# Products of q' with the carried state inside the attention run's row tiles, for six of twelve pairs

## Chip, cores and metric

The kernel runs on one core of one Trainium2 chip. The metric is device time in microseconds. Three runs of the kernel before the change gave 177.44 us (median), 176.88 us (lowest) and 177.53 us (highest).

## What is computed

A gated linear recurrence over four batches, eight heads, 768 steps and 48 columns per head, and then a two-layer network with a tanh GELU:

```python
for t in range(S):
    state = alpha[:, :, t, :, None] * state + einsum('bhd,bhe->bhde', k[:, :, t], v[:, :, t])
    y[:, :, t] = einsum('bhd,bhde->bhe', q[:, :, t], state)
x = y.transpose(0, 2, 1, 3).reshape(3072, 384)
out = gelu_tanh(x @ w_in) @ w_out          # w_in 384 x 2048, w_out 2048 x 384
```

## The kernel before

The sequence is cut into six chunks of 128 steps. A *pair* is one chunk of two batches, called units 0 and 1; there are twelve pairs, numbered 0 to 11 (pair m is chunk m // 2, batches 0 and 1 or 2 and 3). In a pair the recurrence becomes matrix products:

- `ln` (ScalarE) takes the logarithm of alpha, `cum` (TensorE, L378 and L380) sums it down the chunk, `b`, `binv` and `bend` (ScalarE, L407, L401) are exponentials of the sums and of their ends. `qp` = q·b and `kp` = k·binv (VectorE, L418) are q' and k'.
- q' and k' are transposed, by TensorE (L428) and a copy (`ev`, L446) in pairs 0 to 6 and by DMA from SP's queue (`turn`, L466) in pairs 7 to 11. The result `qkT` holds two heads on its 128 partitions: the even head of a couple on partitions 0 to 63, the odd one on 64 to 127.
- `attn` (L489) multiplies k' by q', one matmul for each head and unit. Each uses 64 rows of the array, the upper or the lower half, and the two halves alternate; 16 matmuls in a pair. `mask` (VectorE, L496) applies the triangle: four instructions in a pair, each one bank.
- `y` makes the result of one unit: for chunks after the first, four matmuls of 128 rows by 96 columns of q' with the carried state (L543), then eight of 48 columns of the masked products with v (L546), which add to the same bank. The state tile holds two heads on its partitions and two blocks of 48 columns, with zeros where head and block differ.
- `x` copies a unit's result out of PSUM (L553, on ScalarE or VectorE). It is transposed by TensorE (`tx`, L560, and `xe`, L564) or from pair 6 on by DMA (L472).
- `kv` (L506) and `st` (VectorE, L528 and L531) make the next state; the last chunk needs none.
- The network follows pair by pair: `l1` (layer 1, L572; eight steps of six matmuls, `hT`), `gelu` (ScalarE, L578) and `l2` (layer 2, L591; four steps of four matmuls for each unit, `acc`), `ot` (copy out, L603) and a store from SP's queue (L616). Exponentials and GELU need different tables in ScalarE, so there is a table load on either side of each pair's eight `gelu`.

PSUM's eight banks are shared out as `ca` (one buffer of two banks: `cum`, and the products of one unit in `attn`), `yk` (two banks: `y`, `kv` and everything that TensorE transposes) and `ff` (four banks, taken in turn: `hT`, `acc`, and the products of the other unit). A buffer is taken again only when its last reader has finished.

The order of each engine's instructions is fixed when the program is built. A planner in the kernel (class `Scheduler`) gives each task a cost, a priority and the buffers that it takes, and always puts the task next that can start first; the first part of the order is written out by hand (`FIRST`). TensorE, ScalarE, VectorE and the queues then run their lists strictly in order and wait by semaphores.

In the late part of the kernel, before the change, TensorE's list for one pair reads: seven `l1` steps of an earlier pair, `attn`, the eighth `l1` step, two `l2` steps, `y` of unit 0, one `l2` step, `y` of unit 1, one `l2` step, `cum` of the pair after the one of `attn`, four `l2` steps.

Of the kernel before, what the change touches and what calls it, by code (L numbers as in the profile page):

```python
# [7 lines left out]
F32 = mybir.dt.float32  # L8
# [38 lines left out]
class Scheduler:  # L47
# [16 lines left out]
    def order(self):  # L64
        free = {e: 0 for e in LAT}
        taken = {tag: [] for tag in self.bufs}
        table, wire, xbar, head, out = LN_EXP, 0, 0, 0, []
        left = {e: sorted((t for t in self.tasks if e in t.cost), key=lambda t: t.prio) for e in LAT}

        def given(tag):  # L70

            n, at = len(taken[tag]) - self.bufs[tag], 0
            for u in taken[tag][n] if n >= 0 else ():
                if u.done is None:
                    return None
                at = max(at, u.done)
            return at

        def ready(t, inorder=True):
            if inorder and t.stream not in (None, head):  # L80
                return None
            at = 0
            for d in t.deps:
                if d.done is None:
                    return None
                at = max(at, d.done)
            for tag, _ in t.takes:
                g = given(tag)
                if g is None:
                    return None  # L90
                at = max(at, g)
            return at

        def put(t, at, e):
            nonlocal wire, xbar
            for tag, users in t.takes:
                taken[tag].append(users)
            cost, lat = COST.get((e, t.kind), (t.cost[e], LAT[e])) if fixed and not 300 <= t.prio < 10000 else (t.cost[e], LAT[e])
            t.start, t.end, t.engine, t.load = at, at + cost, e, None
            free[e] = t.end  # L100
            t.done = t.end + lat
            if t.name in self.landed:
                t.done = self.landed[t.name]
                if e != "SP":
                    wire = t.done - W["receipt"]
            elif t.land is not None:
                wire = max(wire, t.end + W["lead"]) + t.land
                t.done = wire + W["receipt_hw" if e == "SP" else "receipt"]
            if t.kind in ("turn", "store"):
                xbar = t.done = max(xbar, t.end + W["landed"] - t.xbar) + t.xbar  # L110
                t.done += t.late
            out.append(t)

        def go(at, e, t):
            nonlocal table, head
            if e == "PE" and not fixed and self.fill and at < self.until and at - free[e] > 300:
                g = given("ff")
                n = int((at - max(free[e], g if g is not None else at) - 60) * 0.95 // W["fill"])
                if n > 0:
                    f = Task("fill", {"PE": n * W["fill"]}, 0, self.fill(n))  # L120
                    put(f.take("ff", f), max(free[e], g), e)
            put(t, at, e)
            if t.table not in (None, table):
                table = t.load = t.table
            for q in t.cost:
                left[q].remove(t)
            if t.stream is not None:
                head = min((x.stream for x in left["PE"] if x.stream is not None), default=None)

        fixed = True  # L130
        for step in self.first:
            e, name = step.split(":")
            if name[:5] == "fill.":
                n = int(name[5:])
                f = Task("fill", {"PE": n * W["fill"]}, 0, self.fill(n))
                at = given("ff")
                assert at is not None, "no bank for idle products"
                put(f.take("ff", f), max(free["PE"], at), "PE")
                continue
            e, t = {"P": "PE", "V": "DVE", "A": "ACT", "G": "POOL", "S": "SP"}[e], self.named[name]  # L140
            at = ready(t, False)
            assert at is not None, f"{name} can't go yet"
            go(max(at, free[e] + (W["table"] if t.table not in (None, table) else 0)), e, t)
        fixed = False
        while any(left.values()):
            best = None
            for e in LAT:
                found = []
                for t in left[e]:
                    at = ready(t)  # L150
                    if at is not None:
                        turn = W["table"] if t.table not in (None, table) else 0
                        at = max(at, free[e] + turn)
                        found.append((at, t, at - turn))
                if found:
                    window = min(f[2] for f in found) + 60
                    at, t, _ = min((f for f in found if f[2] <= window), key=lambda f: (f[1].prio, f[0]))
                    if best is None or at < best[0]:
                        best = at, e, t
            assert best is not None, "no task can go on"  # L160
            go(*best)
        return out
# [9 lines left out]
class _Kernel:  # L172
# [38 lines left out]
    TURN_QK, TURN_X = (7, 8, 9, 10, 11), (6, 7, 8, 9, 10, 11)  # L211

    EV_ACT = (0, 1, 2, 3)

    AT_FF, SINGLE = {0: (1,), 1: (), 2: ()}, (0, 1, 2)

# [254 lines left out]
    def turn_x_dma(self, u, i, c, b):  # L471
        return lambda e: self.nc.sync.dma_start_transpose(self.xT[c % self.NX][:, :, b, :], u["x", i])  # L472

    def attn(self, u, units, apart):
        nc, H, C = self.nc, self.H, self.C

        def emit(e):
            for i in units:
                if i in apart:
                    u["at", i] = [self.tile("ff", [C, H // 2, C], F32, "at") for _ in range(2)]  # L480
                else:
                    at = self.tile("ca", [C, 2, H // 2, C], F32, "at")
                    u["at", i] = [at[:, 0], at[:, 1]]
            for i in units:
                t, at = u["T"][:, :, i], u["at", i]
                for p in range(H // 2):
                    for o in range(2):
                        sl = slice(64 * o, 64 * o + 64)
                        nc.tensor.matmul(at[o][:, p, :], t[sl, 1, p, :], t[sl, 0, p, :], start=True, stop=True)  # L489
        return emit  # L490
# [44 lines left out]
    def y(self, u, i, c, b):  # L535
        nc, H, C, D = self.nc, self.H, self.C, self.D

        def emit(e):
# [6 lines left out]
            for h in range(H):  # L545
                nc.tensor.matmul(y[:, h, :], u["atm", i][:, h % 2, h // 2, :], u["vb"][:, i, h, :],  # L546
                                 start=c == 0, stop=True, skip_group_check=True)
        return emit

    def x(self, u, i):  # L550
# [66 lines left out]


    def tasks(self):
        s = self.s = Scheduler(self.BUFS, self.fill, 60000, self.FIRST, self.LANDED)  # L620
        B, NCH = self.B, self.NCH
        NP = B // 2
        self.p = {(c, i): {} for c in range(NCH) for i in range(NP)}
# [47 lines left out]
        for m, (c, i) in enumerate(pairs):  # L671
# [29 lines left out]
            for r, users in (("a", lns[m]), ("q", qp), ("k", kp)):  # L701
                loads[r, m, 0].take(r, *users)
            lns[m][0].take("la", *cums)
            if m - 1 in self.URGENT:
                cums[0].deps += ats[m - 1]
            if m in self.CUM_FF:
# [17 lines left out]
            for j in range(2):  # L724
# [17 lines left out]
                if m in self.SINGLE or j:  # L742
                    units = (j,) if m in self.SINGLE else (0, 1)
                    apart = self.AT_FF.get(m, (0,))
                    at = s.add("attn", {"PE": W["attn" if len(units) == 1 else "attn2"]}, o + 1, self.attn(u, units, apart), sum(turns[units[0]:], []))
                    ats.setdefault(m, []).append(at)
                    for w in units:
                        ms = masks[w] = [s.add("mask", {"DVE": W["mask"]}, P + 12 + 3 * w, self.mask(u, w, h), [at]) for h in range(2)]
# [4 lines left out]
            for j in range(2):  # L753
                b, o, k, ms, turned = 2 * i + j, P + 10 + 3 * j, kp[j], masks[j], turns[j]
                at = ats[m][-1 if m not in self.SINGLE else j]
                y = s.add("y", {"PE": W["intra"] + (W["inter"] if c else 0)}, P + 20 + j, self.y(u, j, c, b),
                          ms + turned + [vin[j]] + ([states[b, c - 1]] if c else []))
                xc = s.add("x", {"ACT": W["xc_act"], "DVE": W["xc"]}, P + 20 + j, self.x(u, j), [y])
                if m in self.TURN_X:
                    xe = tx = s.add("turn", {"SP": W["turn"]}, P + 22 + j, self.turn_x_dma(u, j, c, b), [xc], xbar=W["xbar_x"], late=W["late_x"] * (m < 6))  # L760
                else:
                    tx = s.add("tx", {"PE": W["tx"]}, P + 22 + j, self.turn_x(u, j), [xc])
                    xe = s.add("xe", {"DVE": W["xe"]}, P + 22 + j, self.turned_x(u, j, c, b), [tx])
                    tx.take("yk", xe)
                y.take("yk", xc)
                xc.take("x", tx)
                users += [at, y]
                ms[0].take("atm", y)
                xts[c, b], ys[b, c] = xe, y
# [1 line left out]
                if c < NCH - 1:  # L771
                    if u["packed"]:
# [2 lines left out]
                        tb.take("yk", k)  # L775
                        users.append(tb)
                        backs.append(tb)
                    kv = s.add("kv", {"PE": W["kv"]}, P + 30 + j, self.kv(u, j), [k, vin[j]])
                    st = states[b, c] = s.add("st", {"DVE": W["st" if c else "st0"]}, P + 30 + j, self.carry(u, j, c, b),
                                              [kv, end] + ([states[b, c - 1], ys[b, c - 1]] if c else []))  # L780
                    kv.take("yk", st)
# [139 lines left out]
```

## Time and profile before

| | before |
|---|---|
| median of three runs | 177.44 us (176.88 to 177.53) |
| span of the profiled execution | 175.3 us |
| TensorE busy | 170.4 us, 97% |
| ScalarE busy | 128.9 us, 74% |
| VectorE busy | 96.8 us, 55% |
| matmuls | 1845 |
| q' by state, L543, 128x96 | 80 matmuls, 6.7 us busy |
| masked products by v, L546, 128x48 | 192 matmuls, 8.7 us busy |
| attention products, L489, 64 rows, 128 columns | 192 matmuls, 8.0 us busy |

The profiled execution's own time is given as its span, 175.3 us from the first instruction to the last; the median of the runs is 2.1 us longer, for what lies around the span. Busy time of a matmul holds its way through the array, and matmuls overlap, so what a matmul costs TensorE's list is read from start to start in the timeline, not from its duration.

### The profile page before, as it was taken

The numbers are of one execution on the slowest core, as the hardware profiler recorded it, in microseconds if no ns is written. First come the engines' busy times: TensorE is split into PE (matmuls) and PEld (weight loads), VectorE is DVE, ScalarE is ACT, GpSimd is POOL, SyncE is SP. The second block draws the span as 40 slices with busy tenths as digits, with TensorE's granted clock in tenths as the row PEclk, the third lists the DMA queues.
The fourth block names the chain that finished last, engine by engine and source line by source line (L and its number), as shares of the span: only waits on it lengthen the run. The fifth ranks groups of instructions, "written<-read, shape, count | busy, mean of one in ns | idle before, by whom it ended". The sixth has DMA issues, their size and how long they took to land.

```text
span 175.3 us, 4440 instructions
## 1 busy us (share of the span) xinstructions
PE 170.4 (97%) x1845; PEld 135.4 (77%) x1845; DVE 96.8 (55%) x192; ACT 128.9 (74%) x213; POOL 57.7 (33%) x64
## 2 busy tenths in 40 slices
PE   7989999999999999999999999999999999999993
PEld 2667999667987896797798698698697697796973
DVE  6499920356888993795598897495426405000000
ACT  4677999666968668768788967977987984481941
POOL 2496348977645776576720000000000000000000
PEclk9999999999999999999999999999999999999999
DMA  4999999999999999999999992271271360401102
GB/s 138 307 262 224 210 243 238 246 205 207 249 273 204 242 256 220 217 226 199 200 264 224 200 136 80 54 172 52 47 187 28 90 165 4 115 20 49 45 0 90
DMA packets 49620, 28.86 MB, mean 165 GB/s; under 512 B 37696, under 2 KB 46016, under 8 KB 49600
## 3 DMA queue, kind: packets, MB, share of 16 engines
q0 software_dynamic: 26464, 17.70, 60.8%
q1 hardware_dynamic: 22592, 10.49, 24.8%
q10 hardware_dynamic: 544, 0.39, 0.8%
q8 instruction: 14, 0.23, 0.6%
q14 instruction: 6, 0.05, 0.1%
HBM read 25.17 MB, written 4.72 MB: 170 GB/s over the span
## 4 chain that ended last, share of the span: by engine, by line
PE 90%; DMA 6%; DVE 1%; issue 0%; ACT 0%; SPq 0%; POOL 0%
PE hT L572 36%; PE acc L591 36%; DMA v<-in_v_dram 4%; PE at L489 4%; PE qkT_ps L428 3%; PE yps L546 3%; PE kv L506 2%; PE yps L543 2%; DMA a<-in_alpha_dram 2%; PE cum L378 2%; PE xT_ps L560 1%; PE cum L380 1%; SPq L305 0%; ACT qkT L446 0%; DVE vb L389 0%
## 5 line engine op out<-in xcount | busy, mean ns | idle before, releaser
L572 PE MATMUL hT<-xT,w_in 128*128 128x256 bf16 x576 | 69.4, 273 | 0.0
L578 ACT ACTIVATE gT<-hT 128x512 bf16<-128x512 f32 x96 | 56.3, 600 | 17.7 <-PE hT L572 14.2
L591 PE MATMUL acc<-w_out,gT 128*128 128x384 bf16 (+3 forms) x416 | 69.0, 313 | 0.0
L572 PEld LDWEIGHTS <-w_in 128*128 128x128 bf16 x576 | 61.1, 114 | 1.6
L591 PEld LDWEIGHTS <-gT 128*128 128x128 bf16 x416 | 36.9, 98 | 19.2
L496 DVE TENSOR_TENSOR atm<-at,ut 128x512 bf16<-128x512 f32 x48 | 30.1, 681 | 12.7 <-PE at L489 12.6
L418 DVE TENSOR_TENSOR qp<-q,b 128x768 bf16<-128x768 f32 (+1 forms) x15 | 11.9, 794 | 14.0 <-ACT b L407 11.7
L418 DVE TENSOR_TENSOR kp<-k,binv 128x768 bf16<-128x768 f32 (+1 forms) x15 | 11.9, 791 | 10.6 <-ACT binv L407 10.6
L603 ACT COPY ot<-acc 128x384 f32<-128x384 f32 (+3 forms) x17 | 7.4, 439 | 13.0 <-PE acc L591 12.9
L308 POOL DMA_DIRECT2D k<-in_k_dram x11 | 12.2, 1107 | 6.6 <-DVE atm L496 3.0
L308 POOL DMA_DIRECT2D vb<-in_v_dram x11 | 12.1, 1102 | 6.7 <-PE hT L572 1.7
L308 POOL DMA_DIRECT2D q<-in_q_dram x11 | 12.2, 1109 | 6.1 <-DVE atm L496 1.3
L308 POOL DMA_DIRECT2D a<-in_alpha_dram x11 | 12.2, 1114 | 5.9 <-DMA w_in<-in_moe_w_in_dram 1.3
L407 ACT ACTIVATE b<-cum 128x768 bf16<-128x768 f32 (+1 forms) x15 | 10.3, 683 | 3.6 <-PE cum L380 2.3
L280 ACT ACT_TABLE_LOAD x9 | 11.5, 1283 | 0.9 <-PEq L905 0.7
L578 ACT ACT_TABLE_LOAD x9 | 11.5, 1283 | 0.2
L407 ACT ACTIVATE binv<-cum 128x768 bf16<-128x768 f32 (+1 forms) x15 | 10.2, 681 | 0.1
L528 DVE TENSOR_TENSOR stmp<-kv,st 128x384 f32<-128x384 f32 x16 | 8.8, 552 | 2.0 <-PE kv L506 2.0
L553 DVE CAST x<-yps 128x384 bf16<-128x384 f32 x12 | 6.7, 556 | 4.7 <-PE yps L546 4.7
L531 DVE TENSOR_TENSOR st<-stmp,ends 128x384 bf16<-128x384 f32 x16 | 8.9, 558 | 0.6
L446 ACT COPY qkT<-qkT_ps 128x512 bf16<-128x512 bf16 (+1 forms) x9 | 6.5, 728 | 3.7 <-PE qkT_ps L428 3.5
L546 PE MATMUL yps<-vb,atm 128*128 128x48 bf16 x192 | 8.7, 183 | 0.4 <-DVE vb L389 0.4
(65 smaller groups left out, 156.7 us busy)
## 6 DMA issues: line engine op xcount, KB each, us to landing
out_dram<-ot SPq DMA_DIRECT2D x19, 192.0 KB, 5.2
a<-in_alpha_dram POOLq DMA_DIRECT2D x9, 384.0 KB, 12.5
q<-in_q_dram POOLq DMA_DIRECT2D x9, 384.0 KB, 11.6
k<-in_k_dram POOLq DMA_DIRECT2D x9, 384.0 KB, 11.7
vb<-in_v_dram POOLq DMA_DIRECT2D x9, 192.0 KB, 11.6
w_in<-in_moe_w_in_dram POOLq DMA_DIRECT2D x4, 384.0 KB, 9.3
w_out<-in_moe_w_out_dram POOLq DMA_DIRECT2D x4, 384.0 KB, 11.1
out_dram<-ot SPq DMA_DIRECT2D x9, 96.0 KB, 1.8
```

What stands on the lines that cost most here:

```text
L280: nc.scalar.add_instruction(mybir.InstLoadActFuncSet(name=nc.get_next_instruction_name(), act_func_set_id=i, engine=mybir.EngineType.Activ ...
L308: dma(u[t][:, lo:hi].rearrange("t b h d -> t (b h) d"), src.rearrange("b h s d -> s (b h) d")[c * C:(c + 1) * C])
L407: self.nc.scalar.activation(u[n].rearrange("t i h d -> t i (h d)")[:, lo:hi], cum, AF.Exp, scale=1.0 if n == "b" else -1.0)
L418: self.nc.vector.tensor_tensor(out, rows, b, op=ALU.mult)
L496: self.nc.vector.tensor_tensor(u["atm", i][:, o], u["at", i][o], self.ut[:, None, :].to_broadcast([self.C, self.H // 2, self.C]), op=ALU.mult)
L528: nc.vector.tensor_tensor(s, acc, old, op=ALU.add)
L531: nc.vector.tensor_tensor(new.rearrange("f p (o d) -> f (p o) d", o=2), acc.rearrange("f p (o d) -> f (p o) d", o=2), ends, op=ALU.mult)
L546: nc.tensor.matmul(y[:, h, :], u["atm", i][:, h % 2, h // 2, :], u["vb"][:, i, h, :], start=c == 0, stop=True, skip_group_check=True)
L572: self.nc.tensor.matmul(h[:, s], w_in[:, j, nt % 4 + s], self.xT[c % self.NX][:, j, lo:hi].rearrange("p g t -> p (g t)"), start=j == 0, st ...
L578: return lambda e: self.nc.scalar.activation(self.gT[c % self.NG][:, nt:nt + 2, lo * self.C:hi * self.C], f.pop(("h", c, lo, nt)), AF.Gelu ...
L591: self.nc.tensor.matmul(f["acc", c, b][:, lo:hi], self.gT[c % self.NG][:, nt, b * self.C:(b + 1) * self.C], self.w_out[:, nt, lo:hi], star ...
L603: self.copy(e)(f["ot", c, b][:, sl], f["acc", c, b] if half is None else f["acc", c, b, half][:, sl])
```

## The change

In pairs 4, 5, 8, 9, 10 and 11 the products of q' with the carried state leave `y` and stand at the head of the `attn` run, for both units at once. They use half of the array's rows each, like the attention products, and multiply one head by its own 48 columns of the state; so four matmuls of 128 rows and 96 columns per unit become eight of 64 rows and 48 columns. Results of even heads go to one `yk` bank and those of odd heads to the other, both units side by side. `y` becomes one run of 16 matmuls that adds the masked products of both units; `x` copies one bank per instruction, that is, all even or all odd heads of both units, into a tile for the pair.

Around it: `attn` of these pairs takes both `yk` banks and waits for the states; `cum` of pairs 9, 10 and 11 goes ahead of `attn` of the pair before; `kv` of pairs 4 and 5 comes after `y`; the planner looks at the second buffer of a kind that a task takes, and stops putting idle matmuls in after 40 us of its own reckoning and not 60 us.

The order that results: nothing differs before `attn` of pair 4, and the number of idle matmuls is the same. TensorE's list for a late pair becomes: `attn` (with the 16 new matmuls ahead of its 16), five `l1` steps of the pair before, `y` of both units (16 matmuls), three `l1` steps, five `l2` steps, `cum`, three `l2` steps. In pairs 4 and 5 `attn` stands after the third `l1` step, the other five follow, then `y`, two `l2` steps, both `tx`, one `l2` step, both `kv`. `attn` of pair 11 comes two `l1` steps after `y` of pair 10, and `y` of pair 11 after one more `l1` step and four `l2` steps. On ScalarE one `x` copy now stands between the fifth and the sixth `gelu` in pairs 8 to 10, after the eighth in pairs 4 and 5, and between two `ot` in pair 11 (the other copy is VectorE's), and three `ot` copies move there from VectorE. The number of table loads is the same. On SP's queue transposes of x move behind those of q' and k' of the next pair.

```diff
+    CARRIED = (4, 5, 8, 9, 10, 11)
+    AHEAD = (9, 10, 11)
+    LATE_KV = (4, 5)
...
+    def carried(self, u, c, b):
+        nc, H, D = self.nc, self.H, self.D
+        u["y"] = [self.tile("yk", [self.C, 2, H // 2, D], F32, "yps") for _ in range(2)]
+        for i in range(2):
+            for p in range(H // 2):
+                for o in range(2):
+                    sl = slice(64 * o, 64 * o + 64)
+                    nc.tensor.matmul(u["y"][o][:, i, p, :], u["T"][sl, 0, i, p, :], self.state[b + i][c % 2][sl, p, o * D:o * D + D],
+                                     start=i == p == 0, stop=False, skip_group_check=True)
...
-    def attn(self, u, units, apart):
+    def attn(self, u, units, apart, carried=None):
...
+            if carried:
+                self.carried(u, *carried)
             for i in units:
                 t, at = u["T"][:, :, i], u["at", i]
...
+    def y_pair(self, u):
+        def emit(e):
+            for i in range(2):
+                for h in range(self.H):
+                    self.nc.tensor.matmul(u["y"][h % 2][:, i, h // 2, :], u["atm", i][:, h % 2, h // 2, :], u["vb"][:, i, h, :],
+                                          start=False, stop=True, skip_group_check=True)
+        return emit
+
+    def x_part(self, u, o):
+        def emit(e):
+            if "xs" not in u:
+                u["xs"] = self.tile("x", [self.C, 2, self.H // 2, 2, self.D], BF16, "x")
+                for i in range(2):
+                    u["x", i] = u["xs"][:, i].rearrange("t p o d -> t (p o d)")
+            self.copy(e)(u["xs"][:, :, :, o], u["y"][o])
+        return emit
...
-        s = self.s = Scheduler(self.BUFS, self.fill, 60000, self.FIRST, self.LANDED)
+        s = self.s = Scheduler(self.BUFS, self.fill, 40000, self.FIRST, self.LANDED)
...
+            if m in self.AHEAD:
+                for t in ats[m - 1]:
+                    t.deps += cums
...
-                    at = s.add("attn", {"PE": W["attn" if len(units) == 1 else "attn2"]}, o + 1, self.attn(u, units, apart), sum(turns[units[0]:], []))
+                    carried = (c, 2 * i) if m in self.CARRIED else None
+                    at = s.add("attn", {"PE": W["attn" if len(units) == 1 else "attn2"] + (230 if carried else 0)}, o + 1, self.attn(u, units, apart, carried),
+                               sum(turns[units[0]:], []) + ([states[2 * i + w, c - 1] for w in units] if carried else []))
...
+                if m in self.CARRIED:
+                    if j == 0:
+                        y = s.add("y", {"PE": 2 * W["intra"]}, P + 20, self.y_pair(u), masks[0] + masks[1] + vin + [at])
+                        xcs = [s.add("x", {"ACT": W["xc_act"], "DVE": W["xc"]}, P + 20 + o, self.x_part(u, o), [y]) for o in range(2)]
+                        at.take("yk", xcs[0]).take("yk", xcs[1])
...
-                    kv = s.add("kv", {"PE": W["kv"]}, P + 30 + j, self.kv(u, j), [k, vin[j]])
+                    kv = s.add("kv", {"PE": W["kv"]}, P + 30 + j, self.kv(u, j), [k, vin[j]] + ([y] if m in self.LATE_KV else []))
```

More of the change, by code (lines that the diff above doesn't have):

```diff
@@ L68, in order, with given @@
         left = {e: sorted((t for t in self.tasks if e in t.cost), key=lambda t: t.prio) for e in LAT}
-        def given(tag):
-            n, at = len(taken[tag]) - self.bufs[tag], 0
+        def given(tag, ahead=0):
+            n, at = len(taken[tag]) + ahead - self.bufs[tag], 0
             for u in taken[tag][n] if n >= 0 else ():
@@ L86, in ready @@
                 at = max(at, d.done)
-            for tag, _ in t.takes:
-                g = given(tag)
+            for k, (tag, _) in enumerate(t.takes):
+                g = given(tag, sum(x[0] == tag for x in t.takes[:k]))
                 if g is None:
                     return None
-                at = max(at, g)
+                at = max(at, given(tag) if tag == "ff" else g)
             return at
@@ L755, in tasks @@
                 at = ats[m][-1 if m not in self.SINGLE else j]
-                y = s.add("y", {"PE": W["intra"] + (W["inter"] if c else 0)}, P + 20 + j, self.y(u, j, c, b),
-                          ms + turned + [vin[j]] + ([states[b, c - 1]] if c else []))
-                xc = s.add("x", {"ACT": W["xc_act"], "DVE": W["xc"]}, P + 20 + j, self.x(u, j), [y])
+                if m in self.CARRIED:
[3 more added lines that the diff above has]
+                        at.take("yk", xcs[0]).take("yk", xcs[1])
+                else:
+                    y = s.add("y", {"PE": W["intra"] + (W["inter"] if c and m not in self.CARRIED else 0)}, P + 20 + j, self.y(u, j, c, b),
+                              ms + turned + [vin[j]] + ([states[b, c - 1]] if c else []))
+                    xcs = [s.add("x", {"ACT": W["xc_act"], "DVE": W["xc"]}, P + 20 + j, self.x(u, j), [y])]
+                    y.take("yk", xcs[0])
                 if m in self.TURN_X:
-                    xe = tx = s.add("turn", {"SP": W["turn"]}, P + 22 + j, self.turn_x_dma(u, j, c, b), [xc], xbar=W["xbar_x"], late=W["late_x"] * (m < 6))
+                    xe = tx = s.add("turn", {"SP": W["turn"]}, P + 22 + j, self.turn_x_dma(u, j, c, b), xcs, xbar=W["xbar_x"], late=W["late_x"] * (m < 6))
                 else:
-                    tx = s.add("tx", {"PE": W["tx"]}, P + 22 + j, self.turn_x(u, j), [xc])
+                    tx = s.add("tx", {"PE": W["tx"]}, P + 22 + j, self.turn_x(u, j), xcs)
                     xe = s.add("xe", {"DVE": W["xe"]}, P + 22 + j, self.turned_x(u, j, c, b), [tx])
                     tx.take("yk", xe)
-                y.take("yk", xc)
-                xc.take("x", tx)
+                if m in self.CARRIED:
+                    txs = (txs if j else []) + [tx]
+                    if j:
+                        xcs[0].take("x", *txs)
+                else:
+                    xcs[0].take("x", tx)
                 users += [at, y]
```

## The prediction

> **What bounds the kernel now.** I began with the clock and span, then the busy tenths and the chain that ended last on the page.
>
> ```profile
> PE   7989999999999999999999999999999999999993
> ...
> PEclk9999999999999999999999999999999999999999
> ...
> PE 90%; DMA 6%; DVE 1%; issue 0%; ACT 0%; SPq 0%; POOL 0%
> ```
>
> TensorE is busy in every slice after the first few at the full granted clock, and the chain is 90% its own work. A busy PE can still hide pauses, so the next view is its timeline over one late pair, in which every start can be set against the matmuls ahead of it.
>
> ```profile
> 127.48 4.75 PE L572 MATMUL hT<-xT,w_in 128*128 128x256 bf16 x42
> 132.16 0.62 PE L489 MATMUL at<-qkT 64*128 64x128 bf16 x16
> 132.71 0.84 PE L572 MATMUL hT<-xT,w_in 128*128 128x256 bf16 x6
> 133.40 1.46 PE L591 MATMUL acc<-w_out,gT 128*128 128x384 bf16 x8
> 134.70 0.33 PE L543 MATMUL yps<-st,qkT 128*128 128x96 bf16 x4
> 134.87 0.36 PE L546 MATMUL yps<-vb,atm 128*128 128x48 bf16 x8
> 135.07 0.81 PE L591 MATMUL acc<-w_out,gT 128*128 128x384 bf16 x4
> ...
> 136.74 0.49 PE L378 MATMUL cum<-la,ut_h 128*128 128x384 f16 x2
> ```
>
> Read start to start. Eight acc take 1.30 us (162 ns each), four products with the state 0.17 us (42 ns each), eight with v 0.20 us (25 ns each). Forty-two hT take 4.68 us; at the 109 ns that each costs elsewhere (18 in 1.96 us at 62.21) that is 0.10 us too much, the price of entering the half-row mode. Nothing else is left over: in this pair TensorE waits for nothing, and the same sums hold in the other pairs after 55 us. So the time changes by what TensorE's list gains or loses, plus any wait that is new.
>
> Two more places of the timeline say what the new matmuls may cost. The first pair of rows answers a window around 144.33 us, the second one around 144.42 us; the third shows one-column matmuls.
>
> ```profile
> 144.35 0.23 PE L489 MATMUL at<-qkT 64*128 64x128 bf16 x2
> ```
>
> ```profile
> 144.35 0.29 PE L489 MATMUL at<-qkT 64*128 64x128 bf16 x4
> ```
>
> ```profile
> 83.30 0.24 PE L380 MATMUL cum<-ones,la 128*128 128x1 f16 x4
> 83.40 0.32 PE L378 MATMUL cum<-la,ut_h 128*128 128x384 f16 x1
> ```
>
> A single such product lasts 216 to 227 ns, and two together take 0.23 us: the upper and the lower half start within a few ns of each other. The next two are done 0.06 us later. So couples follow each other at 56 ns (16 in 0.55 us, of which eight couples are 0.45 us and leaving the mode 0.10 us). One-column matmuls, by contrast, start every 25 ns, as the 48-column ones do: a floor that does not depend on size, but one that two halves of the array do not share, or the couple would not start together.
>
> **The change, part by part.**
>
> *Removed.* Eight products of 96 columns a pair: 2 x 0.17 = 0.335 us of TensorE's list, all on the path.
>
> *Added.* Sixteen products of half the rows and 48 columns, as eight couples. By the floor a couple takes 25 ns; by the trace's only half-row run 56 ns, but that is for 128 columns, and 48/128 of it is 21 ns. If halves did not overlap when this short, 16 x 25 ns = 0.40 us; if loading weights sets the 56 ns, 8 x 56 = 0.45 us. The ends are 0.17 and 0.45 us. I take 0.21 us (26 ns a couple), because the nearest rows are the 48-column run (same width, 25 ns) and the couple that starts together. They stand directly ahead of the 16 attention products in the same mode, so the entering and leaving, 0.10 us each, are paid once as before.
>
> A rule of the Trainium skill speaks against this: TensorEngine Tiling (Array Packing), Instruction Overhead, says that each matmul carries some 60 cycles whatever its width, and that one should not take a tiling factor from a dimension that is already small. Twice as many matmuls, all below 60 columns, would by that alone cost twice eight floors, an estimate of 0.40 us from that page; the trace has the same floor (25 ns at one column), but the row of two matmuls that start together is what I set against the rest.
>
> *y.* Two runs of eight with v (0.205 us each; the first after a wider one is a little dearer) become one run of 16, 16 x 25 = 0.40 us: 0.01 us less. That the banks alternate costs nothing in the attention run, which alternates banks too.
>
> *After attn.* In pairs 4 and 5 an hT now follows the half-row run where a kv did. Six hT behind such a run take 0.69 us (132.71 to 133.40), 0.03 us above 6 x 109 ns; twice, 0.06 us.
>
> *Moved on TensorE* (cum, kv, tx, l1 and l2 steps): no work added.
>
> *Copies.* x has the same 384 elements an instruction (0.56 us on VectorE, 0.48 us on ScalarE), now written in runs of 48. Price nothing on the path if the slack below holds.
>
> *New waits.* I walk one late pair from the end of its last hT, H (133.40 in the rows), with these rows of ScalarE:
>
> ```profile
> 133.60 0.60 ACT L578 ACTIVATE gT<-hT 128x512 bf16<-128x512 f32 x1 [0.73 <-PE hT L572]
> 134.21 1.28 ACT L280 ACT_TABLE_LOAD   x1
> 135.50 0.84 ACT L361 ACTIVATE la<-a 128x768 f16<-128x768 f32 x1
> ...
> 138.03 0.81 ACT L407 ACTIVATE binv<-cum 128x768 bf16<-128x768 f32 x1
> ...
> 138.86 1.28 ACT L578 ACT_TABLE_LOAD   x1
> ```
>
> ln ends at H+2.94. cum now stands behind five l2 steps, at H+3.25: 0.3 us of slack, which has to cover ScalarE's signal. cum ends at H+3.58, b starts 0.2 later, binv ends at H+5.3 (with bend, in one pair, H+5.5). attn starts at H+3.58+3x0.65 = H+5.53, and its second unit, which needs the buffer that cum held, 0.5 us later: 0.5 us of slack or more. The ot that came to ScalarE runs to H+6.2, the table load to H+7.5; the first hT, after attn, is done at about H+7.1, so the first gelu is some 0.2 us late. It has to be done when the fifth hT takes that bank, at H+9.0, and ends at H+8.1; gelu gains 0.05 us a step. VectorE does qp and kp until H+6.45, then four masks at 0.60 us: the first is out before the third hT wants its bank (H+7.1 against H+7.7), the last at H+8.9, and y comes at H+9.7. The x copy between two gelu (0.48 us) fits, since y's 0.40 us delays the next hT as well. Behind a waiting attn all of l1 would queue, and gelu behind that.
>
> Three tighter places: attn of pair 11 comes two l1 steps (1.3 us) after y of pair 10 and needs both yk banks; the later copy ends about 0.9 us after y. In pairs 4 and 5 the transposes of x need ScalarE's copy 1.3 us after y, out about 0.9 us after; the second kv follows the second xe by about 0.1 us. Losing that cover costs a tenth or two, once or twice. SP's queue: transposes of x are wanted a whole pair (12 us) later and take 1.2 us to issue and 2.3 us to land, so going behind q' and k' is free. Three ot leave VectorE, idle almost half of the time.
>
> *Sum.* Per pair 0.21 - 0.335 - 0.01 = -0.135 us; six pairs -0.81; plus 0.06: -0.75 us. The span of 175.3 us becomes 174.55, and the median, 2.1 us above it, 177.44 - 0.75 = 176.7 us. With a couple at 21 ns it is 176.45, with the halves one after the other 177.8, with 56 ns a couple 178.1.
>
> **Rivals.**
>
> *Halves do not gain* (the 0.40 or 0.45 us above): per pair +0.055 or +0.105 us, with the 0.06 together +0.4 to +0.7 us: 177.8 to 178.1 us. Against it: couples that start together. For it: no half-row run this short is in the trace, and every matmul loads its weights.
>
> *attn waits for its banks* (the slower side). It now needs both yk banks, two ff banks and ca at once, and in pairs 8 to 10 the next pair's cum holds ca until ScalarE has read it. ScalarE is busy 10.5 us of the 12.2 us pair (window 127.5 to 139.7) and gets one ot more, so if it falls behind, attn and everything behind it stand still. Slack is 0.5 us; beyond it each us late is a us in each of three pairs. It decides from about 0.25 us of waiting in each of the three (that eats the gain) and makes the kernel slower by over 0.5% from 0.55 us each, ScalarE over 1 us late. At 0.8 us each: +1.65, 179.1 us. For it: many tight places on one in-order list. Against: the walk finds none late.
>
> *The change does not shorten the list*: the products are not what a late pair waits on, ScalarE is, and saved time becomes idle: 177.4 us. Against it: ScalarE waits for hT today (0.73 us ahead of the gelu at 133.60).
>
> **How the numbers follow.** 0.5% is 0.89 us, about what a measurement of this kernel can tell from no change. The forecast has 0.70; its 0.75 us lies just inside that bound, and the 21 ns end or the runs' own spread (0.65 us over three) puts about 0.30 of this beyond it, 0.40 inside. Halves without gain 0.12, all within 0.5%. No shortening 0.04. Waits 0.14, slower. Together faster 0.30, same 0.56, slower 0.14. The range leaves out the waits and little else: from 176.2 (the 21 ns end less 0.25 us of spread) to 178.2. The forecast's own range is 176.2 to 177.1.
>
> **What would show it.** After the change the timeline should show 16 yps of 64 rows by 48 columns in about 0.21 us, then the 16 at, and l1 after 0.55 us; 16 yps in 0.40 us later; no idle time of TensorE in pairs 4 to 11; pairs 9 to 11 about 0.13 us shorter than 12.2 us. A gap ahead of at or of the first yps shows the second rival; 0.40 us for the first 16 shows the first. A gain of more than 1.1 us would mean that something other than these products got cheaper, and I have not seen it.

## The result, and the profile after

| | before | after |
|---|---|---|
| median of ten runs each, side by side | 177.29 us (176.88 to 179.56) | 178.57 us (177.8 to 182.48) |
| ratio | | 1.0071 [1.0046, 1.0095] |
| span of the profiled execution | 175.3 us | 176.0 us |

The change makes the kernel slower by 0.7%; 178.57 us lies above the top of the forecast range, 178.2 us. The profiled execution of the changed kernel was the fastest of its ten (177.8 us), so its profile shows the loss at its smallest, and the run of 182.48 us is not counted in the ratio. In every run of the record the time is 1.8 us above its own span; the 2.1 us given ahead of the prediction compared the profiled execution with the median of others.

First the page after: TensorE's row of the busy tenths, and the chain that ended last.

```profile
PE   7799999999999999999999899999999999999992
...
PE 88%; DMA 6%; ACT 4%; issue 0%; DVE 0%; DVEq 0%
```

One slice in the middle has fallen to 8, and ScalarE has entered the chain. Before going there, the timeline of TensorE over a late pair, with the columns start, duration, engine, line, operation, tiles, shapes and count.

```profile
126.83 0.37 PE L488 MATMUL yps<-st,qkT 64*128 64x48 bf16 x16
127.04 0.61 PE L508 MATMUL at<-qkT 64*128 64x128 bf16 x16
127.58 3.47 PE L608 MATMUL hT<-xT,w_in 128*128 128x256 bf16 x30
130.88 0.56 PE L573 MATMUL yps<-vb,atm 128*128 128x48 bf16 x16
```

Start to start, the sixteen new products take 0.21 us, the attention run 0.54 us, `y` 0.41 us. The next pair's products start at 138.88, so the pair lasts 12.05 us; before, from 127.48 to 139.67, it lasted 12.19 us. That is the forecast's gain of some 0.13 us. The time must have been lost elsewhere. The timeline around 100 us, after and then before:

```profile
97.92 2.76 PE L627 MATMUL acc<-w_out,gT 128*128 128x384 bf16 x16
101.59 0.81 PE L608 MATMUL hT<-xT,w_in 128*128 128x256 bf16 x6 [0.92 <-DMA xT<-x]
```

```profile
98.20 2.76 PE L591 MATMUL acc<-w_out,gT 128*128 128x384 bf16 x16
100.80 0.82 PE L572 MATMUL hT<-xT,w_in 128*128 128x256 bf16 x6
```

The sixteen `acc` need 2.60 us start to start before, 3.67 after: 1.07 us are lost waiting for `xT<-x`. These six `hT` are layer 1's first step for pair 6, the first pair whose x is transposed by DMA. The chain, cut to the stretch that ends there:

```profile
96.35 5.20 DMA xT<-x
101.55 0.04 issue
101.59 0.49 PE hT L608 x3
```

The second unit's transpose was issued at 96.35 us and landed 5.20 us later. Before, it was issued at 96.44 and landed 3.80 us later, at 100.24, and TensorE wanted it at 100.80: 0.56 us of slack. Issued no later, landed 1.3 us later.

The DMA view from 99.4 to 101.8 us says why. It has 40 slices of 0.06 us; the row is what all queues moved in each.

```profile
GB/s 294 282 514 265 273 286 260 269 273 282 77 4 0 0 0 0 0 0 0 4 4 9 9 9 9 13 4 13 9 13 9 9 13 137 273 290 303 273 294 290
...
q8 instruction: 1, 0.02, 2.8%
```

The transposes run at some 270 GB/s. At 99.56 us one packet of 16,384 bytes comes in on q8, the queue that loads instructions (the spike of 514). Its record lasts about 1.05 us. From 100.05 us on nothing moves for half a microsecond, then some 10 GB/s, and only from 101.4 us on the full rate, although the transposes are unfinished: a halt of about 1.4 us. Before the change this stretch holds no such packet; it comes 3 us later, at 102.59 us, and the window from 102.4 to 105.2 us (slices of 0.07 us) shows the same halt:

```profile
GB/s 59 7 234 0 0 29 117 241 271 274 271 274 263 88 18 0 0 0 0 0 0 0 0 7 11 7 7 11 7 11 11 7 11 7 80 263 289 293 293 293
...
q8 instruction: 1, 0.02, 3.2%
```

The short pause around the spike is that between two transposes; the next one, that of k' of pair 8, starts at 102.8 us, stops at 103.4 and goes on at 104.8. It takes 4.45 us from issue to landing instead of some 2.75, and nobody waits for it. So the halt is not new; its place is.

Before, the packets follow each other at every 249 TensorE instructions on average (210 to 292 from one to the next). Up to this point the changed kernel has 32 more of them (8 more matmuls in each of pairs 4 and 5, each with its weight load). This packet starts at TensorE's 2259th instruction before and at its 2237th after, of which 32 are new, so it meets work that lies 54 instructions, or 3 us, earlier. The packets do not all move alike: the next one starts 1.4 us later than before the change (112.5 against 111.1), the fourteenth 5.5 us earlier (156.6 against 162.1). In all there are 48 more matmuls, and fifteen packets where there were fourteen. The last comes at 172.3 us, among the last stores. The DMA view from 172 to 176 us, after and then before (slices of 0.1 us):

```profile
GB/s 338 338 256 0 0 0 0 0 146 315 292 169 16 8 8 8 15 8 0 0 87 287 236 46 0 123 174 31 0 0 0 0 0 0 0 0 0 0 0 0
```

```profile
GB/s 0 0 0 0 0 92 300 346 215 31 0 0 0 97 287 226 46 0 120 180 28 0 0 0 0 0 0 0 0 0 0 0 0 0 0 0 0 0 0 0
```

The pause ahead of the store of 96 KB is in both. But after the change this store ends in a trickle of some 8 GB/s from 173.2 to 173.8 us, and lands 2.4 us after its issue, not 1.6. From the last `ot` copy to the end of the span it takes 2.86 us, against 2.44 before.

So the account is: the matmuls −0.81 us up to pair 10 (whose first `hT` starts at 151.53 before and 151.80 after, that is −0.81 + 1.08; read directly, 0.28 of it ahead of the sixteen `acc` above and 0.52 behind pair 6's first `hT`), the wait for x of pair 6 +1.08, the last stores +0.42: +0.69 us, where the spans differ by 0.68.

### The profile page after: what moved, and what is told of

It is laid out like the page before. It is cut to its first block, busy times and chain, and to the rows that moved or that the text cites. A ratio compares the mean times of both kernels' runs of the same rounds, so it can differ in the third digit from the quotient of the medians.

```text
span 176.0 us, 4532 instructions
## 1 busy us (share of the span) xinstructions
PE 169.3 (96%) x1893; PEld 134.1 (76%) x1893; DVE 94.7 (54%) x188; ACT 129.6 (74%) x217; POOL 57.8 (33%) x64
## 4 chain that ended last, share of the span: by engine, by line
PE 88%; DMA 6%; ACT 4%; issue 0%; DVE 0%; DVEq 0%
PE hT L608 36%; PE acc L627 33%; PE qkT_ps L434 4%; PE at L508 4%; DMA k<-in_k_dram 3%; DMA xT<-x 3%; PE cum L384 2%; PE kv L525 2%; PE yps L573 1%; ACT L286 1%; PE yps L565 1%; PE xT_ps L596 1%; PE yps L488 1%; PE yps L562 1%; ACT qkT L452 1%; PE k_ps L460 1%
## 5 line engine op out<-in xcount | busy, mean ns | idle before, releaser
L627 PE MATMUL acc<-w_out,gT 128*128 128x384 bf16 (+3 forms) x416 | 67.8, 313 | 0.0
L639 ACT COPY ot<-acc 128x384 f32<-128x384 f32 (+3 forms) x20 | 8.8, 443 | 15.6 <-PE acc L627 15.6
L367 ACT ACTIVATE la<-a 128x768 f16<-128x768 f32 (+1 forms) x11 | 8.5, 785 | 0.1
L583 DVE CAST x<-yps 128x384 bf16<-128x384 f32 x6 | 3.3, 557 | 8.7 <-PE yps L573 8.7
```

Of the source, the lines that this page charges most:

```text
L367: self.nc.scalar.activation(u["la"][:, lo:hi, :, 0:self.D], u["a"][:, lo:hi], AF.Ln)
L627: self.nc.tensor.matmul(f["acc", c, b][:, lo:hi], self.gT[c % self.NG][:, nt, b * self.C:(b + 1) * self.C], self.w_out[:, nt, lo:hi], star ...
L639: self.copy(e)(f["ot", c, b][:, sl], f["acc", c, b] if half is None else f["acc", c, b, half][:, sl])
```

## Experiments

The expectations number the theories and say what each holds. The account above, that the added instructions move the instruction packets onto transfers that TensorE is about to need (Theory 3 in them), was formed only after the first four runs; those ask where the wait arises. Each kernel was timed in five rounds beside the kernel before on the same chip.

**The same kernel again**, to see whether the wait is always there.

> The changed kernel once more (one comment more), for a second profile and ten more times. Theory 1 (the transposes of x of pair 6 land late by DMA, TensorE waits ahead of the first layer-1 step of pair 6, and the 0.3 us saved in pairs 4 and 5 is lost there): again 178 to 179 us, and a gap of TensorE of 0.5 to 2.5 us at about 100 us, no other gap over 0.1 us. Theory 2 (the new order of the late pairs brings waits that the first profile did not catch, since its run was the fastest of ten): gaps after 110 us.

178.49 us against 177.30, ratio 1.0049 [1.0018, 1.0081]. The wait is there again and larger, 1.40 us start to start, with the packet at 99.5 us and the landing at 101.4.

**Only the late pairs**: the new products in pairs 8 to 11, none in 4 and 5.

```diff
-    CARRIED = (4, 5, 8, 9, 10, 11)
+    CARRIED = (8, 9, 10, 11)
-    LATE_KV = (4, 5)
+    LATE_KV = ()
```

> Only pairs 8 to 11 have the products inside the attention run; pairs 4 and 5 are as before the change. Theory 1: the place at 100 us is as before the change, with no gap or one under 0.3 us, and four pairs at 0.135 us less make it 0.5 us faster than before, 176.8 us. Theory 2: the late pairs' waits stay, 178 to 178.5 us.

176.49 us against 177.30, ratio 0.9949 [0.9918, 0.9979]: faster than both kernels. The timeline at the place of the wait shows none:

```profile
97.82 2.76 PE L627 MATMUL acc<-w_out,gT 128*128 128x384 bf16 x16
100.42 0.82 PE L608 MATMUL hT<-xT,w_in 128*128 128x256 bf16 x6
```

With no instruction added ahead of pair 6 the packet is at 102.4 us, as before the change, and x lands at 100.4. From pair 4's `attn` to pair 10's first `hT` TensorE's list takes 89.54 us instead of 90.05: 0.52 us less, where four pairs at 0.135 make 0.54. There are fourteen packets, and none at the end. The median falls by 0.81 us, more than the list does; the ratio's interval, 0.37 to 1.45 us, holds both.

**Only pairs 4 and 5.**

```diff
-    CARRIED = (4, 5, 8, 9, 10, 11)
-    AHEAD = (9, 10, 11)
+    CARRIED = (4, 5)
+    AHEAD = ()
```

> Only pairs 4 and 5 have them; pairs 8 to 11 are as before the change. Theory 1: 0.3 us saved ahead of 98 us, a gap of 0.3 us or more at about 100 us, so no gain: 177.3 to 178.3 us. Theory 2: no new waits, 0.2 us faster than before, 177.1 us.

178.47 us against 177.30, ratio 1.0046 [1.0014, 1.0077], a little above the range expected. TensorE waits 0.83 us for pair 6's x, landing at 101.4 with the packet at 99.4. These two pairs alone make the kernel slower, although the spot where it shows lies after them.

**Pair 6's x through TensorE**, as in pairs 0 to 5, in the changed kernel.

```diff
-    TURN_QK, TURN_X = (7, 8, 9, 10, 11), (6, 7, 8, 9, 10, 11)
+    TURN_QK, TURN_X = (7, 8, 9, 10, 11), (7, 8, 9, 10, 11)
```

> The changed kernel, but x of pair 6 is transposed by TensorE and a copy, not by DMA: 6 matmuls of 128 columns more on TensorE's list, 0.33 us. Theory 1: the gap at 100 us is gone, and the six pairs' 0.75 us less 0.33 us is left: 176.9 us. Theory 2: the waits of the late pairs stay, 178 us or more.

177.70 us against 177.30, ratio 1.0027 [1.0000, 1.0054]. The wait at 100 us is gone, but the gain is not what Theory 1 expected. The timeline shows where it went:

```profile
103.33 0.62 PE L508 MATMUL at<-qkT 64*128 64x128 bf16 x16 [1.22 <-DMA qkT<-kp]
```

`attn` of pair 7 now waits for its transposed k'; the packet lies at 101.2 us, among those. (The profiled execution took 179.05 us, so its wait may be longer than that of most.) The transfers of pair 6 were only the first to be hit: putting the wait down to them was half right. Between 99 and 170 us the timelines of these four kernels mark no other idle time of TensorE, so none of the waits is for a bank or a copy.

**Moving the packet without the change.** The first try replaced the first seven idle matmuls of 512 columns by 23 of 156, in the kernel before, as 32 more TensorE instructions at the same number of columns.

```diff
-            for _ in range(n):
-                self.nc.tensor.matmul(ps, self.zero[:, 0:self.C], self.zero, start=True, stop=True)
+            k, w = (23, 156) if n == 7 else (n, 512)
+            for _ in range(k):
+                self.nc.tensor.matmul(ps[:, 0:w], self.zero[:, 0:self.C], self.zero[:, 0:w], start=True, stop=True)
```

> The kernel before the change, but the first seven idle matmuls (512 columns each) are 23 of 156 columns: 32 more instructions on TensorE's list (16 weight loads, 16 matmuls) in time that is idle anyway, all else the same. Pairs 4 and 5 of the changed kernel add just as many ahead of pair 6. Theory 3 (the 16 KiB packet of the instruction queue at 102.6 us comes about 3 us earlier, as it does after the change, and the transposes of x of pair 6 land 1.2 us later for it): slower by 0.8 to 1.2 us, 178.1 to 178.5 us, with a gap of TensorE at about 101 us. Theory 1 as first stated (TensorE merely arrives earlier than the transposes, which go at the pace of the loads): no change, 177.3 us.

178.33 us against 177.16, ratio 1.0065 [1.0048, 1.0082], but not for the reason that was to be tested: the start lost 2.2 us, so TensorE came to pair 6 after its x (1.9 us later than before, at 102.66 us). The second `cum` run of the start, before and in this kernel:

```profile
5.83 1.06 PE L346 MATMUL cum<-la,ut_blk 128*128 128x384 f16 x7
```

```profile
6.43 1.44 PE L347 MATMUL cum<-la,ut_blk 128*128 128x384 f16 x7 [0.54 <-ACT la L360]
```

TensorE waited for `la`, which ScalarE could start at 5.86 us and not at 5.04, when its alpha had landed; the next step came 1.24 us after the start of these seven in place of 0.90, and the first attention run at 10.97 us in place of 8.76. Whether the narrower idle matmuls had a part in the late load isn't shown, and the profiled execution (178.96 us) is the longest of the six. As a test of Theory 3 this run says nothing.

**More idle matmuls in the changed kernel**: 71 of 48 columns, and 39 of 92, in place of the seven (the same lines, other numbers).

> The changed kernel, but the first seven idle matmuls are 71 of 48 columns: 128 more instructions on TensorE's list at the start, which moves the instruction packets by half their distance of some 11 us, away from the transposes of x of pair 6. Theory 3: packets at about 89 and 106 us, the gap at 100 us under 0.3 us, and the gain that the sum gave comes through: 176.4 to 176.8 us. Theory 1 as first stated: the gap stays, 178 us or more. The start may be up to 0.4 us later, since narrow matmuls may not run at the rate of wide ones.

177.59 us against 177.16, ratio 1.0015 [0.9988, 1.0043]. No wait at 100 us, but in the profiled execution (179.01 us, the longest of the twelve) the start is nearly 3 us late, so TensorE comes after the landing in any case. How much the packet's place gave can't be told.

> The same with 39 of 92 columns, 64 more instructions. Theory 3: the packet comes about 4 us ahead of where the changed kernel has it, at about 95 us, when the transposes of x of pair 6 are on their way too; its hold of about 1 us may fall on the loads still under way or on the transposes, so 176.5 to 178 us, and the landing of the second transpose of x, less where the packet came, says which. Theory 1: as the changed kernel, 178.5 us.

178.12 us against 177.16, ratio 1.0049 [1.0027, 1.0071], just above the range expected. Here the start is as usual, and the packet, at 97.9 us, lies on the same transposes:

```profile
102.16 0.60 PE L609 MATMUL hT<-xT,w_in 128*128 128x256 bf16 x4 [1.35 <-DMA xT<-x]
```

Moving the packet by 1.7 us was not enough to clear them.

**Moving the packet where it costs nothing.** Idle matmuls at the start were the wrong place. The sixteen layer-2 matmuls of one unit (chunk 1, batch 0), in the kernel before, become two of 192 columns each: 32 more TensorE instructions for about 0.04 us, well ahead of pair 6, and all else as it was.

```diff
+            halves = (c, b) in ((1, 0),)
+            if halves:
+                for nt in range(part * 4, part * 4 + 4):
+                    for lo in (0, 192):
+                        self.nc.tensor.matmul(f["acc", c, b][:, lo:lo + 192], self.gT[c % self.NG][:, nt, b * self.C:(b + 1) * self.C],
+                                              self.w_out[:, nt, lo:lo + 192], start=nt == 0 and lo == 0, stop=nt == self.NFT - 1,
+                                              skip_group_check=True)
...
```

> The kernel before the change, with each of the 16 layer-2 matmuls of one unit (chunk 1, batch 0, run at about 52 to 57 us) split in two of 192 columns: 32 more instructions on TensorE's list at the price of some 0.05 us, the start left alone. Pairs 4 and 5 of the changed kernel add as many. Theory 3 (the 16 KiB packet of instructions then falls at about 99.5 us instead of 102.6 us and holds the transposes of x of pair 6 back): slower by 0.8 to 1.2 us, about 178.3 us, a gap of TensorE at about 100.8 us of 0.5 us or more. Theory 1 as first stated (only how early TensorE arrives counts): no change, 177.2 us.

178.31 us against 177.29, ratio 1.0068 [1.0042, 1.0094]. The products are those of the kernel before, and the loss is about as large as that of the change. That the two ratios nearly agree is chance: this kernel has neither the 0.81 us gained nor the longer tail. Timeline, then the DMA view from 99.4 to 101.8 us:

```profile
98.51 2.44 PE L598 MATMUL acc<-w_out,gT 128*128 128x384 bf16 x14
101.78 0.49 PE L572 MATMUL hT<-xT,w_in 128*128 128x256 bf16 x3 [0.83 <-DMA xT<-x]
```

```profile
GB/s 282 277 307 290 286 245 533 269 269 286 265 269 269 154 9 0 0 0 0 0 0 0 0 4 9 9 9 9 9 9 13 9 9 9 13 13 111 273 286 299
```

The packet has come 3 us earlier, to 99.76 us, and the transposes stop behind it until 101.6 us. This is the run that shows Theory 3: nothing but these sixteen matmuls, 32 instructions more, was changed, and TensorE is as early at pair 6 as before (its sixteen `acc` start at 98.18 us, before at 98.20).

The same in the kernel with only the late pairs (same lines, L634 in place of L598):

> The kernel with the products inside the attention run in pairs 8 to 11 alone (176.5 us), with one unit split, 32 more instructions. Theory 3: the packet at 99.5 us again, a gap at about 100.5 us, 177.4 to 178 us. Theory 1: no change, 176.5 us.

178.11 us against 177.29, ratio 1.0053 [1.0035, 1.0070]: the fastest kernel has lost its gain to 32 instructions.

```profile
101.91 0.27 PE L608 MATMUL hT<-xT,w_in 128*128 128x256 bf16 x1 [1.33 <-DMA xT<-x]
```

**Moving it further.** Four units split (chunk 1, all batches), 128 more instructions, in the kernel before and in the changed one.

> The kernel before the change with four units (chunk 1) split like this, 128 more instructions. Theory 3: packets move by half their distance, away from the transposes of pair 6, so no gap; 64 more matmuls cost 0.1 to 0.2 us: 177.2 to 177.4 us. Theory 1: the same.

179.33 us against 177.29, ratio 1.0120 [1.0097, 1.0142], a miss. Packets now lie at 96.7, 128.9 and 143.3 us, each on transposes that are wanted soon: 0.71 us are lost ahead of pair 6's layer 1, and 0.83 and 0.75 us ahead of `attn` of pairs 10 and 11. One of these:

```profile
133.71 0.45 PE L489 MATMUL at<-qkT 64*128 64x128 bf16 x10 [0.77 <-DMA qkT<-kp]
```

The expectation had looked at one packet. All of them move.

> The changed kernel with the same four units split, 128 more instructions. Theory 3: the packet moves from 99.5 to about 95 us, the gap at 100 us is gone or under 0.3 us, and the gain of 0.75 us less 0.1 to 0.2 us comes through: 176.5 to 176.8 us. Theory 1: the gap stays, 178.5 us.

177.24 us against 177.29, ratio 0.9998 [0.9979, 1.0016], again a miss. The packet is at 95.1 us, still among the transposes, and another lies on those of pair 11 (139.75 us, 1.9 us long):

```profile
101.11 0.82 PE L608 MATMUL hT<-xT,w_in 128*128 128x256 bf16 x6 [0.36 <-DMA xT<-x]
```

```profile
144.93 0.62 PE L508 MATMUL at<-qkT 64*128 64x128 bf16 x16 [0.26 <-DMA qkT<-kp]
```

Two waits that cost 0.52 and 0.43 us start to start, in place of one of over 1 us.

**A whole packet.** Seven units split in the changed kernel (chunk 0, batches 0 to 2, and all of chunk 1): 224 instructions, with the change's own 32 just 256, so that the packets lie about where they lay before the change.

> The changed kernel with seven units of layer 2 split (chunk 0, batches 0 to 2, and chunk 1), 224 more instructions: with the 32 of pairs 4 and 5 that makes 256, one whole packet, so the packets fall where they did before the change (and where they fall with pairs 8 to 11 alone changed). 112 more matmuls at 2 to 3 ns each over the wide ones cost about 0.3 us. Theory 3: a packet at about 102.5 us, no gap at 100 us, none in pairs 8 to 11, 176.6 to 177.0 us. If the changed kernel's wait at pair 6 came from pairs 4 and 5 in another way than by the packets, the gap stays: 178.5 us.

176.70 us against 176.91, ratio 0.9984 [0.9967, 1.0002].

```profile
98.86 2.76 PE L634 MATMUL acc<-w_out,gT 128*128 128x384 bf16 x16
101.45 0.82 PE L608 MATMUL hT<-xT,w_in 128*128 128x256 bf16 x6
```

No wait here nor later; the packet is at 102.0 us, x lands at 100.7. All six pairs' products are there, and the loss is gone. The splits themselves cost some 0.3 us, so the version with only the late pairs stays the fastest.

Packet and landing of pair 6's second x side by side, from the records of the traces:

| kernel | packet, us | landing, us | TensorE loses, us |
|---|---|---|---|
| before | 102.6 | 100.2 | 0 |
| late pairs only | 102.4 | 100.4 | 0 |
| changed, seven split | 102.0 | 100.7 | 0 |
| changed | 99.6 | 101.5 | 1.08 |
| changed, again | 99.5 | 101.4 | 1.40 |
| pairs 4 and 5 only | 99.4 | 101.4 | 0.83 |
| before, one split | 99.8 | 101.7 | 1.0 |
| late pairs only, one split | 99.7 | 101.9 | 1.49 |
| changed, 39 idle | 97.9 | 102.1 | 1.51 |
| before, four split | 96.7 | 101.5 | 0.71 |
| changed, four split | 95.1 | 101.1 | 0.52 |

Left out are the kernel without a DMA for pair 6's x and the two whose start was late. Whether the transposes are done by 100.7 or only from 101.1 us on goes by where the packet lies, not by which products the kernel has. The packet of the first two rows starts at TensorE's 2259th instruction; in the five kernels with 32 more instructions ahead of it (changed twice, pairs 4 and 5 only, the two with one split) it starts between the 2231st and the 2239th. And in all fourteen traces together, behind the last loads (from 99 us on), packets of q1, the queue of transposes and stores, take over 0.8 us in 19 places; every one of these begins 0.3 to 1.2 us after the start of an instruction packet.

The stores at the end go the same way: the tail from the last `ot` to the end is 2.84 to 3.04 us in the kernels with a packet at 172.3 to 172.6 us (the changed one twice, pair 6's x through TensorE, late pairs with one split), and 2.42 to 2.45 us in the others. One of these, before with four split, has a packet at 172.2 us too, but ends later: its last matmul starts 2.5 us behind the packet.

## Why the prediction was wrong, point by point

- *Removed and added matmuls: right.* The sixteen half-row products take 0.21 us, the value taken; so halves do overlap at 48 columns, and the first rival falls. TensorEngine Tiling (Array Packing), Instruction Overhead, in the Trainium skill speaks against splitting a small dimension; by its 60 cycles for each matmul the estimate was 0.40 us, and the measurement, at half of that, decides.
- *`y`, and entering and leaving the mode once: right* (0.41 us where 0.40 was taken). Late pairs are 0.13 us shorter, and four of them alone bring 0.52 us.
- *Copies, banks and tight places: right.* No gap of TensorE over 0.1 us follows after 102 us, so the second rival, `attn` waiting for its banks, isn't what made the kernel slower. The third, that saved time becomes idle, falls with the run of the late pairs.
- *New waits, SP's queue: the step that failed.* "Transposes of x are wanted a whole pair (12 us) later and take 1.2 us to issue and 2.3 us to land" was read in late pairs and taken for all. At pair 6, with loads still running beside them until 98.6 us, the second takes 3.80 us to land before the change and has 0.56 us of slack, not a pair; and where an instruction packet falls on it, 5.20 us, with TensorE waiting 1.08. The walk through the waits covered one late pair, and the sentence "in this pair TensorE waits for nothing" was taken to cover the rest without the slack of each DMA being read.
- *The sum: a term was missing.* It priced instructions by TensorE's time alone. Thirty-two instructions, early, also move the later loads of code, the one that matters here by 3 us, and the 96 in all bring one load more: +1.08 and +0.42 us, against −0.81 for the matmuls (−0.75 in the forecast). The slower side was there among the rivals, but with another mechanism.
- A reader could have seen part of it. The view of the transposes of x (line L472) in the kernel before ends with the line below: 2.3 us is the median of twelve, and the longest took 5.9. The page before lists fourteen packets on the instruction queue, and the DMA view shows transposes halted at 103.4 us; nothing waited for these, so nothing pointed there.

```profile
DMA to landing us min/median/max: 2.3/2.3/5.9
```

What stays open: why one packet on the one queue halts all transposes for about 1.4 us (that it does is seen, how it does isn't), and why the packets do not move by equal steps. And the profiles account for 0.68 us, while the medians differ by 1.28; the wait differs from execution to execution (1.08 and 1.40 us in the two that were profiled), but the longer runs have no profile.

## What to carry to other kernels

Where an engine's list is full, added instructions have two prices: their own time, and the shift of the later loads of code. Look for the packets of the instruction queue in the trace and for the DMAs under way in the 1.5 us behind each; where one of these has less than 1.5 us of slack (the largest loss here was 1.51 us), an edit far ahead of it can cost more than it saves, or seem to gain. To tell a change's own effect from this, shift the code by a like number of cheap instructions in the kernel before; here that alone gave 1.0068 where the change gave 1.0071.

## What the runs showed of the hardware

- A load of code of 16 KiB that falls on DMA transposes halts them for about 1.4 us in the three rows above (100.05 to 101.4, 103.4 to 104.8 and 100.2 to 101.6 us), the last 0.8 us of it at some 10 GB/s in place of 270; a wait of 0.4 to 1.5 us followed for TensorE where it needed them soon. The Trainium skill, Runtime: NRT & Kernel Launch, Instruction fetch mechanics, has such blocks (256 instructions, fetched by the sequencer through a DMA queue of its own) and calls the cost of crossing to the next one "mostly hidden". Size and spacing agree with the trace (16,384 bytes, 249 TensorE instructions on average); that it is hidden holds here only for packets that meet no transfer with a short slack.
- DMA transposes of x, all of one size, took 2.3 us to land in most late pairs before the change; the second of pair 6 took 3.8 us beside loads and 5.2 us beside loads and a packet.
- Half-row products of 48 columns cost 13 ns each (96 of them 1.28 us), half of the 25 ns of full-row products of that width.
- In the profiled execution with 71 idle matmuls of 48 columns TensorE stood idle for 1.95 us, up to 7.21 us, waiting for `la`, and the granted clock fell to 0.63 from 8 to 12 us (the number behind the five engines' busy times). What it waited for was a late load; that the narrow matmuls were the cause isn't shown, and with 39 of 92 columns the start was as usual to within 0.3 us:

```profile
8.00:12.00 4.00, 3.76 (x33) 2.27 (x32) 2.37 (x6) 1.53 (x4) 3.59 (x6) 0.63 0.90 246
```
